# Splitting the loads at the end: the last w2 chunk in four loads of 51, 51, 16 and 10 rows

## The chip, the cores and the metric

The kernel runs on one core of a Trainium2 chip. The time is that of the whole program on the device, in microseconds (us); of several runs the median is taken. Beside the times there is a profile of one execution, with a trace of every instruction and of the packets that the core's 16 DMA engines moved.

## The reference

The reference is one decode step of an adaptive-layernorm transformer block: batch 8, one token each, model width 512, all in float32. Attention has 32 query heads over 8 key-value heads of size 128, and looks at the last 2048 positions of a cache of 8192. The second half is a feed-forward block of width 1792 with a squared ReLU.

```python
W = min(4096, max(256, Sk // 4))                       # 2048 positions
q = (x @ wq).reshape(B, Sq, Hq, Dh).transpose(0, 2, 1, 3)
k = repeat(k_cache[:, :, Sk - W:, :], rep, axis=1)
v = repeat(v_cache[:, :, Sk - W:, :], rep, axis=1)
p = softmax(einsum("bhqd,bhkd->bhqk", q, k) * Dh ** -0.5)
attn = einsum("bhqk,bhkd->bhqd", p, v).transpose(...).reshape(B, Sq, Hq * Dh) @ wo
...
mod = silu(c) @ w_mod                                   # sa, ca, ga, sb, cb, gb
x = x + ga * attn(layernorm(x) * (1 + ca) + sa)
h = layernorm(x) * (1 + cb) + sb
r = relu(h @ w1 + b1)
out = x + gb * ((r * r) @ w2 + b2)
```

Nearly all the work is reading: K and V of the window are 134 MB, and the weights some 30 MB more.

## The kernel before

All large operands pass through one SBUF tensor, `home`, that is cut into four slots of 4 MB, and one slot `small` of 2 MB. The list `loads` gives the order: w_mod, wq, then K and V tiles by turns (16 of each, two per key-value head) with three wo tiles between them, then the last two V tiles, `tail` (the last wo tile and half of w1), the other half of w1, and w2. `pump()` issues the next load as soon as a slot of its size is free, and `done()` frees a slot and calls it. All these loads are issued by SP (L105, L110, L124, L128), so they stand in one queue in this order. The framework gives the loads of SP and ACT eight semaphores in turn; a load that comes round to a semaphore waits until the load that had it before has landed. Within a slot a load waits only for the work on the part that it overwrites.

The five small loads of x and c (`xc_in`, L68; the last quarter of the width in two) and the two of the biases b1 and b2 (L503, L504) are issued by ACT.

The loop over `s` does attention in a fixed order: VectorE transposes K tiles (L190), TensorE computes scores (L359), VectorE and ScalarE the softmax, and TensorE multiplies by V (`weighted`, L446), five steps behind. `weighted` takes a V tile in four quarters; the last V tile is loaded as a half and two quarters, so that TensorE may start on each part as it lands. `parts` and `gather` (L463 to L475) bring a head's output into the tile `oT`, and `project_o` (L486) multiplies it by wo.

After the loop everything is one chain. L569 to L595 form the residual x1, the second layernorm and its transposed input; L611 multiplies by w1; L619 to L623 make the squared ReLU, `rT`; L630 multiplies by w2. The product has 14 chunks f of 128 rows of w2 each, and four column groups of 128. Its weight tile holds row 14 p + f of w2 in partition p, chunk f, so that a load of one chunk is 128 partitions of 2 KB. The w2 load is cut along the chunks: 0 to 7, 8 and 9, 10 and 11, 12, 13. A matmul waits only for the load that holds its chunk. `spin(n)` (L566) issues n matmuls on the identity matrix into a PSUM tile that nobody reads; they keep TensorE busy while it would wait. Each float32 matmul of the program shows as two in the profile. L638 and L639 apply the gate and the residual, and L640 stores the result.

Of the kernel before, what the change touches and what calls it, by code (L numbers as in the profile page):

```python
# [19 lines left out]
def tile_adaln_cached_attention_mlp(  # L20
# [14 lines left out]
    nc = tc.nc  # L35
    P = 128
    B, HKV, SK, DH = k_cache.shape
    D = wq.shape[0]
# [25 lines left out]
    nc.vector.memset(xc_in, 0.0)  # L64
    for q in range(D // P):
        b = slice(32 * q, 32 * q + B)
        for x, y in ((0, 2),) if q < 3 else ((0, 1), (1, 2)):
            nc.scalar.dma_start(xc_in[b, x:y], xc[b, x:y])  # L68

    ident = consts.tile([P, P], F32, name="ident")  # L70
# [8 lines left out]
    big = NJ * DH  # L79
# [9 lines left out]
    def size_of(key):  # L89
        return "small" if key[0] in ("wo", "w1") or key == ("mod", 1) else "big"  # L90

    def load(key):
        kind, i = key
        held[key] = free[size_of(key)].pop(0)
        if key == ("wq", 0):
            return
        t = slots[size_of(key)][held[key]]
        if kind in "KV":

            hk, c = divmod(i, 2)  # L100
            v = k_cache[4 * c : 4 * c + 4, hk] if kind == "K" else v_cache[c::2, hk]
            v = v[:, SK - W :, :].rearrange("u (p j) d -> p u (j d)", j=NJ)
            cuts = (0, big // 2, big * 3 // 4, big) if key == ("V", 2 * HKV - 1) else (0, big)
            for x, y in zip(cuts, cuts[1:]):
                nc.sync.dma_start(t[:, x:y], v[..., x:y])  # L105
            return

        def rows(o, v):
            n = v.shape[1] * v.shape[2]
            nc.sync.dma_start(t[:, o : o + n].rearrange("p (a n) -> p a n", n=v.shape[2]), v)  # L110

        w1v = w1.rearrange("(p kc) n -> p kc n", p=P)

        def wo_rows(j):

            r = 2 * REP * DH
            return wo[j * r : (j + 1) * r, :].rearrange("(h p i) n -> p h (i n)", p=P, i=4)

        if kind == "wo":
            rows(0, wo_rows(i))  # L120
        elif kind == "mod":

            v = w_mod.rearrange("(p kc) n -> p (kc n)", p=P)
            nc.sync.dma_start(t, v[:, big:] if i else v[:, :big])  # L124
        elif kind == "wq":

            o = base[held["wq", 0]]
            nc.sync.dma_start(home[:, o : o + 2 * big], wq.rearrange("(p k) n -> p (k n)", p=P))  # L128
        elif kind == "tail":
            rows(0, wo_rows(HKV // 2 - 1))  # L130
            rows(big // 2, w1v[:, 0:2])
        elif kind == "w1":
            rows(0, w1v[:, 2:4])
        else:
            v = w2.rearrange("(p c) n -> p c n", p=P)
            for lo, hi in ((0, 8), (8, 10), (10, 12), (12, 13), (13, 14)):
                rows(D * lo, v[:, lo:hi])

    def slot(key, n, o=0):

        t = slots[size_of(key)][held[key]][:, o:]
        return t[:, : t.shape[1] // n * n].rearrange("p (a n) -> p a n", n=n)
# [9 lines left out]
    def pump():  # L152
        while at[0] < len(loads) and free[size_of(loads[at[0]])]:
            load(loads[at[0]])
            at[0] += 1
# [53 lines left out]
    lo = consts.tile([P, 1], F32, name="lo")  # L209
    hi = consts.tile([P, 1], F32, name="hi")  # L210
# [31 lines left out]
    for k in (2, 3, 4):  # L242
        n = 1 << k
# [27 lines left out]
    for i, last in enumerate((16, 8)):  # L271
        at_ = 0
        while at_ < last:
            kc, m = divmod(16 * i + at_, 6)
            n = min(4 - m if m < 4 else 6 - m, last - at_)
# [234 lines left out]
    for s in range(N + PV_LAG + 1):  # L510
        g, i = divmod(s, C)
        q, h = divmod(s, 2)
        v = s - PV_LAG
# [49 lines left out]
    def spin(n):  # L563

        for _ in range(n):
            nc.tensor.matmul(spin_ps, ident, ident[:, None, :].to_broadcast([P, 4, P]), start=True, stop=True)  # L566
# [57 lines left out]

    py = ps_m.tile([P, 512], F32, name="m_ps", tag="m_ps")
    nc.tensor.matmul(py[:, :P], qsel.rearrange("p q b -> p (q b)"), b2_in, start=True, stop=False)
    spin(3)
    for f in range(FC):
        for q in range(NQ):
            nc.tensor.matmul(  # L630
# [6 lines left out]
    y = work.tile([P, P], F32, name="y", tag="one_y", bufs=1)  # L637
# [39 lines left out]
```

## Time and profile before

| | |
|---|---|
| Time before, median of 3 runs | 393.93 us (393.89 to 394.06) |
| The profiled execution: its own time | 394.02 us |
| Its span, first to last instruction | 392.2 us |
| Mean granted TensorE clock | 0.89 |
| TensorE matmul (PE), busy | 255.1 us, 65% |
| VectorE (DVE), busy | 219.7 us, 56% |
| ScalarE (ACT), busy | 46.3 us, 12% |
| Load queue of SP (q1): bytes, share of 16 engines | 164.70 MB, 98.3% |
| Mean rate over the span | 421 GB/s |

The span lies inside the program's time: the execution took 1.8 us more than its span. Engines are PE (matmul), PEld (weight load of TensorE), DVE, ACT, POOL and SP; a trailing q names the engine's sequencer, which issues DMAs. In the timeline a row has start, duration, engine, line, operation, tiles, count, and in brackets how long the engine had been idle and what ended the idle time. In the windows a row has the stretch, its length, then busy time and count of PE, PEld, DVE, ACT and POOL, then the granted clock, the mean busy share of the 16 DMA engines, and GB/s. In the rows of queues there are packets, MB and share; in those of issues the tiles, the issuing engine, the count, the size of each and, where it is known, the median time from issue to landing; in those of waits who waited for whom, microseconds in total, times, and the longest.

### The profile page before, as it was taken

The numbers are of one execution on the slowest core, as the hardware profiler recorded it, in microseconds if no ns is written. First come the engines' busy times: TensorE is split into PE (matmuls) and PEld (weight loads), VectorE is DVE, ScalarE is ACT, GpSimd is POOL, SyncE is SP. The second block draws the span as 40 slices with busy tenths as digits, with TensorE's granted clock in tenths as the row PEclk, the third lists the DMA queues.
The fourth block names the chain that finished last, engine by engine and source line by source line (L and its number), as shares of the span: only waits on it lengthen the run. The fifth ranks groups of instructions, "written<-read, shape, count | busy, mean of one in ns | idle before, by whom it ended". The sixth has DMA issues, their size and how long they took to land.

```text
span 392.2 us, 4670 instructions
## 1 busy us (share of the span) xinstructions
PE 255.1 (65%) x2006; PEld 77.7 (20%) x2006; DVE 219.7 (56%) x315; ACT 46.3 (12%) x89; POOL 1.3 (0%) x8
## 2 busy tenths in 40 slices
PE   0091958879228973797384837873774828896796
PEld 0030211112002321222021202221221202233324
DVE  1261099889056835783582817780775457855222
ACT  0120011221003100310031003000201003004010
POOL 0000000000000000000000000000000000000000
PEclk9997789989859996999699688999796969998989
DMA  8999999999999999999999999999999999999994
GB/s 329 430 435 439 440 435 431 428 430 401 453 428 428 426 431 428 430 431 446 423 426 435 428 433 435 430 424 431 407 450 431 426 431 436 432 423 408 427 424 178
DMA packets 7685, 165.04 MB, mean 421 GB/s; under 512 B 832, under 2 KB 1008, under 8 KB 1520
## 3 DMA queue, kind: packets, MB, share of 16 engines
q1 hardware_dynamic: 7568, 164.70, 98.3%
q8 instruction: 16, 0.26, 0.3%
q10 hardware_dynamic: 96, 0.04, 0.0%
q14 instruction: 5, 0.04, 0.0%
HBM read 164.67 MB, written 0.07 MB: 420 GB/s over the span
## 4 chain that ended last, share of the span: by engine, by line
DMA 62%; PE 19%; DVE 16%; issue 2%; SPq 0%; ACT 0%; DVEq 0%; ACTq 0%
DMA home<-in_A_k_cache_dram 46%; DVE kT L190 12%; DMA home<-in_A_wq_dram 9%; PE s_ps L359 8%; DMA home<-in_A_wo_dram 7%; PE m_ps L304 3%; PE o_ps L446 2%; PE q_ps L566 1%; DVE pT L425 1%; PE wo_ps L486 1%; PE m_ps L630 1%; PE m_ps L611 1%; PE p_ps L390 1%; DVE qbd L322 1%; DVE pr L418 1%
## 5 line engine op out<-in xcount | busy, mean ns | idle before, releaser
L190 DVE STREAM_TRANSPOSE kT<-home 128x1024 f32<-128x1024 f32 x128 | 151.1, 1219 | 87.0 <-DMA home<-in_A_k_cache_dram 83.6
L359 PE MATMUL s_ps<-kT,qst 128*32 128x512 f32 x512 | 129.4, 1076 | 21.5 <-DVE kT L190 20.6
L446 PE MATMUL o_ps<-home,pT 128*32 128x256 f32 x1024 | 69.8, 396 | 11.1 <-DVE pT L425 9.6
L446 PEld LDWEIGHTS o_ps<-home,pT 128*32 128x32 f32 x1024 | 33.5, 116 | 101.2 <-issue 60.5
L375 PE MATMUL m_ps<-ident,mx 128*1 128x128 f32 x16 | 4.3, 364 | 59.8 <-DVE mx L373 59.8
L359 PEld LDWEIGHTS s_ps<-kT,qst 128*32 128x32 f32 x512 | 14.5, 116 | 41.5 <-DVE kT L190 33.2
L425 DVE STREAM_TRANSPOSE pT<-pr 128x2048 f32<-128x2048 f32 x8 | 18.2, 2272 | 1.0 <-ACT pr L408 1.0
L408 ACT ACTIVATE pr<-pr,own 128x512 f32<-128x512 f32 x16 | 17.9, 1233 | 0.3
L402 ACT ACTIVATE pr<-p_ps,nm 128x512 f32<-128x512 f32 x8 | 5.5, 688 | 97.1 <-DVE nm L399 97.1
L369 ACT COPY ss<-s_ps 128x512 f32<-128x512 f32 x8 | 4.7, 587 | 100.6 <-issue 72.4
L347 ACT COPY qst<-q_ps 32x128 f32<-32x128 f32 x32 | 8.2, 257 | 70.2 <-PE q_ps L336 69.9
L304 PE MATMUL m_ps<-home,h1T 128*32 128x512 f32 x64 | 10.0, 793 | 8.7 <-DMA home<-in_A_wq_dram 8.7
L375 PEld LDWEIGHTS m_ps<-ident,mx 128*1 128x1 f32 x16 | 0.7, 81 | 65.0 <-DVE mx L373 65.0
L224 PE MATMUL m_ps<-xsum,sel 128*128 128x1 f32 x2 | 0.6, 362 | 19.8 <-DVE xsum L222 19.8
L322 DVE COPY qbd<-m_ps 32x128 f32<-32x128 f32 x8 | 3.0, 372 | 18.1 <-PE m_ps L319 18.0
L390 PE MATMUL p_ps<-ss,perm 128*128 128x512 f32 x16 | 11.3, 794 | 0.0
L399 DVE TENSOR_SCALAR nm<-m_ps 128x1 f32<-128x1 f32 x8 | 1.3, 158 | 15.8 <-PE m_ps L395 15.8
L418 DVE TENSOR_SCALAR pr<-pr,own 128x512 f32<-128x512 f32 x16 | 9.2, 657 | 0.8 <-ACT pr L402 0.8
L202 DVE TENSOR_SCALAR e_sb<-e_sb 128x128 f32<-128x128 f32 x1 | 0.2, 226 | 14.4 <-ACT e_sb L201 14.4
L429 PE MATMUL m_ps<-zs,tsel 128*128 128x8 f32 x16 | 2.9, 252 | 8.1 <-DVE zs L420 8.1
L463 DVE TENSOR_SCALAR o_sb<-o_ps,bit 128x128 f32<-128x128 f32 x16 | 4.9, 304 | 4.9 <-PE o_ps L446 4.9
L373 DVE TENSOR_REDUCE mx<-s_ps 128x1 f32<-128x512 f32 x8 | 5.3, 662 | 3.8 <-ACT ss L369 3.8
(124 smaller groups left out, 125.8 us busy)
## 6 DMA issues: line engine op xcount, KB each, us to landing
home<-in_A_k_cache_dram SPq DMA_DIRECT2D x16, 4096.0 KB, 27.0
home<-in_A_v_cache_dram SPq DMA_DIRECT2D x15, 4096.0 KB, 20.0
small<-in_A_wo_dram SPq DMA_DIRECT2D x3, 2048.0 KB, 31.1
home<-in_w_mod_dram SPq DMA_DIRECT2D x1, 4096.0 KB, 12.5
small<-in_w_mod_dram SPq DMA_DIRECT2D x1, 2048.0 KB, 16.9
home<-in_A_v_cache_dram SPq DMA_DIRECT2D x1, 2048.0 KB
home<-in_A_v_cache_dram SPq DMA_DIRECT2D x2, 1024.0 KB, 21.2
home<-in_A_wo_dram SPq DMA_DIRECT2D x1, 2048.0 KB, 25.5
```

The costliest lines, as they stand in the source:

```text
L190: nc.vector.transpose(KTS[q, j][:, rows], k[:, rows, 32 * j : 32 * j + 32])
L304: nc.tensor.matmul(pqs[r][32 * g : 32 * g + 32, :], hT[:, kc, :], w[:, 4 * r + g, :], start=(kc == 0), stop=(kc == NQ - 1),)
L322: nc.vector.tensor_copy(qbd[b, 4 * r : 4 * r + 4, j].rearrange("p g (b t) -> p t g b", t=REP), pT_[b].rearrange("p (t g b) -> p t g b", t= ...
L347: nc.scalar.copy(own[b, :, :, i, 0], pq[b, :P].rearrange("p (c m t) -> p c m t", c=2, t=REP))
L359: nc.tensor.matmul(s_ps[0][32 * g : 32 * g + 32, :], qst[hk % 2][:, P * (4 * c + u) + 32 * j :][:, :32], kT[:, u], start=(c == 0 and j == ...
L373: nc.vector.tensor_reduce(mx, s_ps[0], axis=AX.X, op=ALU.max)
L390: nc.tensor.matmul(sp, perm, SS_.pop(hk), start=True, stop=True)
L402: nc.scalar.activation(pr.rearrange("p j x -> p (j x)"), SS_.pop(hk), AF.Exp, bias=nm, scale=SCALE, accum_out=z)
L408: nc.scalar.mul(X_[hk][..., w], pr, own[:, w : w + 1])
L418: nc.vector.tensor_scalar(X_[hk][..., w], pr, own[:, w : w + 1], None, op0=ALU.mult)
L425: nc.vector.transpose(PT_[hk].rearrange("p e j r -> p j e r"), X_.pop(hk).rearrange("p j x w -> p j (x w)"))
L446: nc.tensor.matmul(O_[n][32 * g : 32 * g + 32, : 2 * DH], PT_[hk][:, e, j : j + 2].rearrange("p j r -> p (j r)"), vt[:, j : j + 2, :].rear ...
```

## The change

Four things change; no arithmetic does.

- The last chunk of w2 (13) is loaded in four loads by partition: rows 0 to 50, 51 to 101, 102 to 117 and 118 to 127. The other chunks come in three loads: 0 to 7, 8 to 11, 12.
- The last V tile is loaded in two halves.
- The last of the four loads of x and c is no longer cut into two.
- `spin(3)` ahead of the w2 product becomes `spin(1)`.

The number of loads in the whole program stays the same: three more for w2's last chunk, one fewer for its other chunks, one fewer for V, one fewer for x and c.

```diff
-        for x, y in ((0, 2),) if q < 3 else ((0, 1), (1, 2)):
+        for x, y in ((0, 2),):
             nc.scalar.dma_start(xc_in[b, x:y], xc[b, x:y])
...
-            cuts = (0, big // 2, big * 3 // 4, big) if key == ("V", 2 * HKV - 1) else (0, big)
+            cuts = (0, big // 2, big) if key == ("V", 2 * HKV - 1) else (0, big)
             for x, y in zip(cuts, cuts[1:]):
                 nc.sync.dma_start(t[:, x:y], v[..., x:y])
...
             v = w2.rearrange("(p c) n -> p c n", p=P)
-            for lo, hi in ((0, 8), (8, 10), (10, 12), (12, 13), (13, 14)):
+            for lo, hi in ((0, 8), (8, 12), (12, 13)):
                 rows(D * lo, v[:, lo:hi])
+            lo = 0
+            for n in (51, 51, 16, 10):
+                nc.sync.dma_start(t[lo : lo + n, D * 13 : D * 14], v[lo : lo + n, 13])
+                lo += n
...
     nc.tensor.matmul(py[:, :P], qsel.rearrange("p q b -> p (q b)"), b2_in, start=True, stop=False)
-    spin(3)
+    spin(1)
```

## The prediction

> **What bounds the kernel now.** I read the queues of the page first, then the busy time by stage for the last microseconds, then the timeline there. The page says that the load queue is nearly always busy:
>
> ```profile
> q1 hardware_dynamic: 7568, 164.70, 98.3%
> q8 instruction: 16, 0.26, 0.3%
> q10 hardware_dynamic: 96, 0.04, 0.0%
> ```
>
> SP's queue (q1) keeps the 16 DMA engines busy for 98.3% of the span, so only its end can be shortened. The windows there give, in the last two columns, the mean busy share of the 16 engines and the rate:
>
> ```profile
> 384.00:385.00 1.00, 1.00 (x4) 0.41 (x3) 0.26 (x1) 0.00 (x0) 0.00 (x0) 1.00 0.98 381
> 385.00:386.00 1.00, 1.00 (x14) 0.35 (x16) 0.00 (x0) 0.00 (x0) 0.00 (x0) 1.00 0.66 262
> 386.00:387.00 1.00, 1.00 (x47) 1.00 (x42) 0.00 (x0) 0.00 (x0) 0.00 (x0) 1.00 0.53 211
> 387.00:388.00 1.00, 1.00 (x48) 1.00 (x42) 0.00 (x0) 0.00 (x0) 0.00 (x0) 1.00 0.49 186
> 388.00:389.00 1.00, 1.00 (x36) 0.58 (x24) 0.00 (x0) 0.00 (x0) 0.00 (x0) 1.00 0.10 20
> ```
>
> The reader is to see that the engines do not finish together. In 387 to 388 the share is 0.49: eight of sixteen still carry data and eight have nothing left. In 385 to 386 the eight that finish early are missing for 0.34 × 16 = 5.4 engine-microseconds, so they end at about 385.3 on average. The last slice holds 0.10 × 16 = 1.6 engine-microseconds, for eight engines 0.2 each: the late ones carry their last byte at about 388.2. So the early half ends about 2.9 us ahead.
>
> The q8 row gives a cause: 16 fetches of instructions, 0.3% of sixteen engines' 392.2 us, or about 1.2 us each on one engine. Two such fetches on each of eight engines make about 2.4 us. Every load gives all sixteen engines the same number of rows, so nothing makes this up again. The timeline of the end:
>
> ```profile
> 382.88 2.84 PE L566 MATMUL q_ps<-ident 128*128 128x512 f32 x6
> 383.98 0.28 DVE L623 SCALAR_TENSOR_TENSOR pr<-relu 128x112 f32<-128x112 f32 x1
> 385.65 3.41 PE L630 MATMUL m_ps<-home,pr 128*32 128x128 f32 x112
> 388.63 0.16 PEld L630 LDWEIGHTS m_ps<-home,pr 128*32 128x32 f32 x8 [0.21 <-DMA home<-in_B_w_dram]
> 389.13 0.29 DVE L638 TENSOR_TENSOR y<-m_ps,modC 128x128 f32<-128x128 f32 x1 [4.87 <-PE m_ps L630]
> 389.77 0.35 SPq L640 DMA_DIRECT2D out_dram<-y  x1
> ```
>
> The w2 product (L630) has its operand at 384.26 (L623) but starts at 385.65, behind the warm-ups of L566. It runs 14 chunks in 3.41 us, 0.244 each, ends at 389.06, and waits for data only ahead of its last chunk: 0.21 us, until the last load is reported at about 388.6, which is 0.4 behind the last byte. Two things thus end almost together, the late engines' data and a product that started late. From 389.06 on everything is a chain that the change leaves alone.
>
> **The change part by part.** First, the early edits. The vector c and x come in four ACT loads instead of five, which shifts by one place the semaphores that loads take in turn:
>
> ```profile
> 1.16 2.03 ACTq L68 DMA_DIRECT2D xc_in<-in_xc_dram  x5
> 1.64 36.69 DMA home<-in_A_wq_dram
> SPq L105 <- DMA home<-in_w_mod_dram: 11.2, 1, 11.2
> ```
>
> One issue of 0.4 us goes, and SP's 11.2 us wait ahead of the first K load moves or disappears; but the chain runs through the wq load until 38.33 whatever was issued behind it. I cost this at nothing; without the wq load as cover it would be worth 0.4 us at most either way.
>
> Second, V's last tile in two loads. PE then gets its third quarter together with its fourth:
>
> ```profile
> 370.05 0.19 DVE L475 TENSOR_TENSOR oT<-tr,rz 128x32 f32<-128x32 f32 x1
> 371.35 2.97 PE L486 MATMUL wo_ps<-home,oT 128*32 128x512 f32 x16 [1.82 <-DMA home<-in_A_wo_dram]
> 119.37 1.07 PE o_ps L446 x16
> ```
>
> A quarter tile is 16 of these matmuls, about 1.1 us by the last row. L475 ends at 370.24, and L486 waits for the wo load until 371.35: 1.1 us of cover, and half of 2.97 more because the first eight of L486's sixteen matmuls belong to the head before. So nothing; without the cover, up to 1.1 us.
>
> Third, two warm-ups fewer. They are four of the six matmuls at L566: 2.84 × 4/6 = 1.9 us. PE is free at about 383.8, and the w2 product may start when its operand is there (384.3) and its first load has landed. Below the last report at 388.6 lie six chunks of eight rows per engine. A row is 2 KB; an engine moves 186/(0.49 × 16) = 23.7 to 262/(0.66 × 16) = 24.8 GB/s, so 0.082 us a row. The first w2 load is therefore reported at 388.6 − 6 × 8 × 0.082 = 384.7. The product can start 0.95 us earlier, but this is worth something only as far as the data allow.
>
> Fourth, chunks 8 to 11 in one load. This is reported at 388.6 − 2 × 8 × 0.082 = 387.3. Behind it PE has six chunks, 6 × 0.244 = 1.46 us, so it cannot end before 388.8. This is a new bound, 0.26 ahead of 389.06.
>
> Fifth, the last chunk as 51, 51, 16 and 10 rows. How many engines does such a load use?
>
> ```profile
> DMA packets 7685, 165.04 MB, mean 421 GB/s; under 512 B 832, under 2 KB 1008, under 8 KB 1520
> xc_in<-in_xc_dram ACTq DMA_DIRECT2D x3, 8.0 KB
> xc_in<-in_xc_dram ACTq DMA_DIRECT2D x2, 4.0 KB
> pr<-in_B_b_dram ACTq DMA_DIRECT2D x1, 7.0 KB
> pr<-in_B_b_dram ACTq DMA_DIRECT2D x1, 2.0 KB
> ```
>
> ACT's seven loads have 5 × 8 + 2 × 4 = 48 rows; their queue, q10, counts 96 packets, so every row brings one closing packet of its own: eight rows went to eight engines, four rows to four. Of the 832 small packets 784 remain, 16 for each of SP's 49 loads. In all these shapes the engines divide the rows evenly. For 51 rows no row of the trace exists. The bounds are one engine (51 rows each time) and sixteen (four at most). The nearest rows have equal shares on at most sixteen engines, and the largest such divisor of 51 is 3: 17 rows each. I take that. [...]
>
> Three engines then carry 17 + 17 + 1 + 1 = 36 rows instead of 8, 28 × 0.082 = 2.3 us more; all others one or two, 0.5 us less. Which three? No view prints engine numbers. I followed the packet records behind the DMA column engine by engine: they run without gaps, so each can be followed, though near neighbours may be mixed up. The engines of the four-row loads are among those of the eight-row loads; three of the four are early and one is late; of the four others at least two are late. If engines are taken in order and the fetches fall on a block of neighbours, the block starts at the fourth engine, and the first three are early. Then they end at 385.3 + 2.3 = 387.6, at the worst of them 388.0, and the others at 388.2 − 0.5 = 387.7. With 0.4 for the report and 0.24 for the chunk, PE ends by this at 388.25 to 388.65, ahead of the bound of 388.8.
>
> The sum: PE ends at 388.8 instead of 389.06, −0.26. The profiled execution took 394.02 us (span 392.2 and 1.8 around it), 0.09 above the median of 393.93; so 393.76 on its scale and 393.7 on that of the runs.
>
> The added issues, three more on SP for the last chunk, wait for older loads:
>
> ```profile
> 378.87 1.71 PE L611 MATMUL m_ps<-home,pr 128*32 128x448 f32 x16
> 361.86 4.88 SPq L110 DMA_DIRECT2D home<-in_B_w_dram  x5
> SPq L110 <- DMA home<-in_A_v_cache_dram: 15.6, 4, 8.8
> SPq L640 <- DMA home<-in_A_wo_dram: 4.6, 1, 4.6
> home<-in_B_w_dram SPq DMA_DIRECT2D x2, 256.0 KB, 22.2
> out_dram<-y SPq DMA_DIRECT2D x1, 64.0 KB, 1.6
> ```
>
> L640 shows it: eight semaphores go round, and the store already waits for the wo load, eight places ahead. Now the sixth and seventh w2 loads would wait for the wo load (371.3) and the first w1 load (in use by L611 at 378.87). Only the store is queued behind them, which needs y at 389. They are issued by about 379, for data due at 387: nothing. A load on an idle queue lands 1.6 us after issue, so the cover is some 6 us.
>
> [...] Here the 22.2 us from issue to landing say that start-up lies under queued data.
>
> **The rivals.** *One of the three is a late engine.* It decides as soon as any of the three is in the half that ends at 388.2. Then 28 rows more end at 388.2 + 2.3 = 390.5, reported at 390.9, PE ends at 391.15: +2.1, or 396.0. For it: half of all engines are late, and one of the four. Against it: the order just described. 0.27.
>
> *The load is spread evenly after all*: at most 4 + 4 + 1 + 1 = 10 rows, 0.16 later, 394.1; the change does not do what it says. 0.05.
>
> *PE becomes slow*: with fewer warm-ups the clock drops, and six chunks at half speed cost 1.46 more: PE ends at 390.3, 1.2 later than before, about 395.1. Against it:
>
> ```profile
> 370.00:372.00 2.00, 0.66 (x8) 0.29 (x12) 0.20 (x2) 0.00 (x0) 0.00 (x0) 1.00 1.06 451
> ```
>
> PE was idle here for 1.3 of 2 us at a granted clock of 1.00; the new gaps are under 1 us. 0.03.
>
> *Each small load pays its own start*, 3 × 1.6 = 4.8: 398.7. 0.02. One engine for 51 rows, 94 × 0.082 = 7.7 more at least: over 401. 0.01.
>
> *The early engines have more room*: if chunks 8 to 11 land 0.6 earlier than I put it, PE ends by the last chunk, and 0.8 is gained: 393.1. 0.04.
>
> **How the numbers follow.** The forecast itself has 0.58. A measurement of this kernel can tell about 0.2%, 0.8 us, from no change. Forecast and even spread are within that: 0.63. Late engine, slow PE, start-up and single engine are slower: 0.33. Faster: 0.04. The forecast's own range is 393.4 to 394.1, from the landing of chunks 8 to 11 (0.3 either way) and the worst early engine. That leaves out more than 2 in 10, so the range goes on to the late engine, 396.2.
>
> **What would show it.** Right: the DMA share in the last 2 us below 0.49 with three engines or fewer in the very end; L630 starting near 384.7, waiting for w2 near 387.3, ending near 388.8; L486 still released by the wo load; two matmuls at L566. Wrong: a DMA share near 3/16 or less for about 2 us with L630 waiting in it, which is a late engine; more than one wait of over 0.5 us ahead of the last chunk; matmuls of L630 longer than before; an SP wait for the first w1 load that lasts beyond 385.

## The result and the profile after

The kernel after takes 395.06 us (median of 10 runs, 394.76 to 395.67), the kernel before 394.06 in the same session (10 runs, 393.89 to 394.35): a ratio of 1.0026, 95% interval 1.0016 to 1.0036. It is slower by 1.0 us, more than the 0.2% that can be told from no change. The forecast was 393.7; the range to 396.2 holds the result. A few single executions, of the kernel before among others, took 397.4 to 398.7 us where the rest of the same kernel's lie near 394; no median rests on them.

The profiled execution took 395.34 us (span 393.4), 1.32 more than the one of before. First the windows of after, with the columns as before (share of the DMA engines and GB/s last):

```profile
385.00:386.00 1.00, 0.69 (x26) 0.72 (x29) 0.00 (x0) 0.00 (x0) 0.00 (x0) 1.00 0.77 258
386.00:387.00 1.00, 1.00 (x48) 1.00 (x39) 0.00 (x0) 0.00 (x0) 0.00 (x0) 1.00 0.68 195
387.00:388.00 1.00, 0.27 (x12) 0.00 (x0) 0.00 (x0) 0.00 (x0) 0.00 (x0) 1.00 0.66 201
388.00:389.00 1.00, 0.81 (x32) 0.81 (x32) 0.00 (x0) 0.00 (x0) 0.00 (x0) 1.00 0.21 64
389.00:390.00 1.00, 0.58 (x24) 0.34 (x17) 0.00 (x0) 0.00 (x0) 0.00 (x0) 1.00 0.09 18
```

The reader is to see the last two columns together. In 386 to 387 the share is 0.68 where it was 0.53: 2.4 engines more are busy, as the prediction wanted of the three that take the rows of the last chunk. But they move 195 GB/s, not 211. A busy engine carries 195/(0.68 × 16) = 17.9 GB/s; before, it was 24.9. More engines work and less arrives. The timeline of the product (L634, where before has L630) and of the store:

```profile
385.31 1.95 PE L634 MATMUL m_ps<-home,pr 128*32 128x128 f32 x64 [1.91 <-DMA home<-in_B_w_dram]
388.19 1.30 PE L634 MATMUL m_ps<-home,pr 128*32 128x128 f32 x40 [0.92 <-DMA home<-in_B_w_dram]
389.91 0.43 PE L634 MATMUL m_ps<-home,pr 128*32 128x128 f32 x8 [0.42 <-DMA home<-in_B_w_dram]
391.04 0.38 SPq L644 DMA_DIRECT2D out_dram<-y  x1
```

PE is idle three times for data: 1.91 us ahead of chunk 0, 0.92 ahead of chunk 8, 0.42 ahead of chunk 13. It ends at 390.34 instead of 389.06, +1.28; the store follows 1.27 later than before. So the whole loss of this execution lies in the landing of w2.

### The profile page after: what moved, and what is told of

Its sections match the earlier page's. It is cut to its first block, busy times and chain, and to the rows that moved or that the text cites. A ratio compares the mean times of both kernels' runs of the same rounds, so it can differ in the third digit from the quotient of the medians.

```text
span 393.4 us, 4662 instructions
## 1 busy us (share of the span) xinstructions
PE 250.1 (64%) x2002; PEld 75.9 (19%) x2002; DVE 219.6 (56%) x315; ACT 46.2 (12%) x89; POOL 1.3 (0%) x8
## 4 chain that ended last, share of the span: by engine, by line
DMA 75%; DVE 12%; PE 11%; issue 1%; SPq 0%; DVEq 0%
DMA home<-in_A_k_cache_dram 55%; DMA home<-in_B_w_dram 11%; DVE kT L194 10%; DMA home<-in_A_wq_dram 9%; PE s_ps L363 7%; PE m_ps L308 2%; PE o_ps L450 2%; DVE qbd L326 1%; DVE o_sb L468 1%; DVE o_sb L467 0%; SPq L124 0%; PE m_ps L323 0%; PE m_ps L634 0%; DVE y L642 0%; DVE y L643 0%
## 5 line engine op out<-in xcount | busy, mean ns | idle before, releaser
L450 PE MATMUL o_ps<-home,pT 128*32 128x256 f32 x1024 | 69.2, 392 | 11.3 <-DVE pT L429 9.6
L308 PE MATMUL m_ps<-home,h1T 128*32 128x512 f32 x64 | 8.6, 700 | 10.6 <-DMA home<-in_A_wq_dram 10.6
```

The costliest lines, as they stand in the source:

```text
L308: nc.tensor.matmul(pqs[r][32 * g : 32 * g + 32, :], hT[:, kc, :], w[:, 4 * r + g, :], start=(kc == 0), stop=(kc == NQ - 1),)
L450: nc.tensor.matmul(O_[n][32 * g : 32 * g + 32, : 2 * DH], PT_[hk][:, e, j : j + 2].rearrange("p j r -> p (j r)"), vt[:, j : j + 2, :].rear ...
```

## The experiments

The theory after the two traces: **shared write side**. DMA engines that write into the same few partitions slow one another, as if they shared something, which the expectation below calls a path. It is the author's guess from the two windows (195 GB/s at a share of 0.68, 211 at 0.53); what would be shared, and by which partitions, they do not show. By it, three engines that carry 102 rows write into partitions that the late engines still write too, and slow them. The rivals: **start-up** (each small load costs something by itself), **merge** (chunks 8 to 11 in one load are to blame), and the warm-ups.

**The parts alone.** First, the kernel before with the split only:

```diff
-            for lo, hi in ((0, 8), (8, 10), (10, 12), (12, 13), (13, 14)):
+            for lo, hi in ((0, 8), (8, 10), (10, 12), (12, 13)):
                 rows(D * lo, v[:, lo:hi])
+            lo = 0
+            for n in (51, 51, 16, 10):
+                nc.sync.dma_start(t[lo : lo + n, D * 13 : D * 14], v[lo : lo + n, 13])
+                lo += n
```

> Kernel before with one edit: the last w2 chunk in four loads of 51, 51, 16 and 10 rows. Shared write side (two or more DMA engines that write into the same few partitions share one path, so the 102 rows of the three engines run at about 0.11 us a row, not 0.082, and the other engines' packets slow down too, as the trace of after shows with 195 GB/s at a share of 0.68 against 211 at 0.53): the last chunk is reported 0.7 to 1.2 us later than before, +0.7 to +1.2 us. Merge (chunks 8 to 11 in one load are to blame): 0, within 0.3. Start-up (each small load costs something by itself): +1.0, as in after.

Measured: 395.34 us (5 runs) against 394.02, ratio 1.0037 (1.0023 to 1.0050): 1.3 us, a little above the range of the theory. Second, the kernel after with chunk 13 in one load, `((0, 8), (8, 12), (12, 13), (13, 14))`:

> Kernel after with the last chunk in one load of 128 rows; everything else of after stays. Shared write side: the last chunk is reported at about 388.6 as before, chunks 8 to 11 at about 387.3, a DMA share and GB/s as in before (0.53 at 211 in 386 to 387); 0 to -0.3 us against before. Merge: +0.7 to +1.2. Start-up: 0 to -0.3, as shared write side.

Measured: 394.22 (11 runs), ratio 1.0006 (0.9997 to 1.0014). Third, the kernel before with `spin(1)` for `spin(3)`:

> Kernel before with one warm-up call instead of three, nothing else. If PE is bound by the last chunk's report at 388.6: 0, within 0.2 us, with the product starting at about 384.7 and a wait for w2 ahead of the last chunks. If the start at 385.65 was part of the bound: -0.3 to -0.6. If fewer warm-ups lower the clock: +1.

Measured: 394.10 (11 runs), ratio 0.9999 (0.9979 to 1.0019). The split makes the whole loss, and the rest of the change is worth nothing that can be measured. Merge falls. The timeline says how the split does it. The kernel with one warm-up, whose product starts early enough to show every landing; these are the waits ahead of chunks 10, 12 and 13:

```profile
387.33 0.38 PEld L630 LDWEIGHTS m_ps<-home,pr 128*32 128x32 f32 x16 [0.27 <-DMA home<-in_B_w_dram]
387.97 0.16 PEld L630 LDWEIGHTS m_ps<-home,pr 128*32 128x32 f32 x8 [0.27 <-DMA home<-in_B_w_dram]
388.61 0.16 PEld L630 LDWEIGHTS m_ps<-home,pr 128*32 128x32 f32 x8 [0.48 <-DMA home<-in_B_w_dram]
```

The same three waits in the kernel with the split alone:

```profile
388.06 0.38 PEld L634 LDWEIGHTS m_ps<-home,pr 128*32 128x32 f32 x16 [0.94 <-DMA home<-in_B_w_dram]
388.76 0.16 PEld L634 LDWEIGHTS m_ps<-home,pr 128*32 128x32 f32 x8 [0.33 <-DMA home<-in_B_w_dram]
389.26 0.19 PEld L634 LDWEIGHTS m_ps<-home,pr 128*32 128x32 f32 x8 [0.34 <-DMA home<-in_B_w_dram]
```

The reader is to see that chunk 13 is not alone: chunks 10 and 11, loaded as before, are 0.73 late, chunk 12 0.79, chunk 13 0.65. These wait for the late engines, which carry no more rows than before. They have been slowed, and the packet records of the traces say so directly: of the 4 KB packets (rows of chunks 8 to 11) that start between 385.5 and 387, the median took 0.20 us with the split alone and 0.16 before.

**Partitions by themselves.** A kernel that only loads: rows of 28 KB, each load waited for before the next, the same rows into different partitions.

```diff
+    def phase(*parts):
+        t = pool.tile([P, 7168], F32, name="t", tag="t")
+        for rows, to in parts:
+            nc.sync.dma_start(t[to], v[rows])
+    phase((slice(0, 8), slice(0, 8)))
+    phase((slice(0, 8), slice(0, 32, 4)))
...
```

> Leaves the whole computation out and stores zeros: twelve loads of 28 KB rows, each waited for before the next, the whole list twice: 128 rows; 8 rows into partitions 0 to 7, into every fourth, into every sixteenth; 16 rows into 0 to 15, into every eighth; 32 rows into 0 to 31, into every fourth; 51 rows into 0 to 50, into every second; 3 rows into 0 to 2, into 0, 4 and 8. An engine alone needs 28.7 KB / 24.9 GB/s = 1.15 us a row, a load on an idle queue lands about 1.7 us after that. [...] No shared write side: 8 rows 2.9 wherever they go, 16 rows 2.9, 32 rows 4.0, 3 rows 2.9. [...]

Its timeline; the bracket is the time from the end of one phase to the landing of the next, in the order of the expectation, from 128 rows to 3 rows side by side:

```profile
11.88 0.14 DVE L53 COPY sink<-t 1x1 f32<-1x1 f32 x1 [10.89 <-DMA t<-in_B_w_dram]
17.60 0.14 DVE L53 COPY sink<-t 1x1 f32<-1x1 f32 x1 [5.58 <-DMA t<-in_B_w_dram]
21.55 0.14 DVE L53 COPY sink<-t 1x1 f32<-1x1 f32 x1 [3.80 <-DMA t<-in_B_w_dram]
26.20 0.14 DVE L53 COPY sink<-t 1x1 f32<-1x1 f32 x1 [4.51 <-DMA t<-in_B_w_dram]
32.21 0.14 DVE L53 COPY sink<-t 1x1 f32<-1x1 f32 x1 [5.87 <-DMA t<-in_B_w_dram]
36.75 0.14 DVE L53 COPY sink<-t 1x1 f32<-1x1 f32 x1 [4.41 <-DMA t<-in_B_w_dram]
43.48 0.14 DVE L53 COPY sink<-t 1x1 f32<-1x1 f32 x1 [6.58 <-DMA t<-in_B_w_dram]
48.58 0.14 DVE L53 COPY sink<-t 1x1 f32<-1x1 f32 x1 [4.96 <-DMA t<-in_B_w_dram]
76.96 0.14 DVE L53 COPY sink<-t 1x1 f32<-1x1 f32 x1 [28.23 <-DMA t<-in_B_w_dram]
100.49 0.14 DVE L53 COPY sink<-t 1x1 f32<-1x1 f32 x1 [23.39 <-DMA t<-in_B_w_dram]
105.41 0.14 DVE L53 COPY sink<-t 1x1 f32<-1x1 f32 x1 [4.78 <-DMA t<-in_B_w_dram]
```

Eight rows take 5.58 us side by side and 3.80 into every fourth partition, but 4.51 into every sixteenth, though those lie further apart. So the partitions alone change the time, and their distance alone does not explain it; which partitions slow one another is not shown. Sixteen rows take 5.87 side by side and 4.41 spread, 32 rows 6.58 and 4.96, three rows 4.78, and 3.50 into partitions 0, 4 and 8. The start costs more than I put (3.80 where 2.9 was expected). Fifty-one rows side by side take 28.23 us, longer than 128 (10.89), and longer than the 21 that 17 rows of 1.15 us behind one another and 1.7 would make; into every second partition they take 23.39. The windows of the two:

```profile
55.00:70.00 15.00, 0.00 (x0) 0.00 (x0) 1.00 0.18 59
80.00:95.00 15.00, 0.00 (x0) 0.00 (x0) 1.00 0.19 75
```

0.18 × 16 = 2.9: about three engines, each at 59/2.9 = 20 GB/s; spread out, 0.19 × 16 = 3.0 engines have 75/3.0 = 25 each.

The second kernel of this kind loads all 128 rows in pieces, queued one behind another.

```diff
+    for n in (7168, 512):
+        for _ in range(2):
+            phase(n, slice(0, 128))
+            phase(n, *blocks(32, 32, 32, 32))
+            phase(n, *combs(4))
+            phase(n, *blocks(64, 64))
+            phase(n, *combs(2))
+            phase(n, *blocks(51, 51, 16, 10))
```

> Leaves the whole computation out and stores zeros: 128 rows loaded six ways, each waited for, the list twice with rows of 28 KB and twice with rows of 2 KB: one load; four blocks of 32; four combs of 32 (every fourth partition); two blocks of 64; two combs of 64; 51, 51, 16 and 10. [...] Rows of 2 KB: 0.66 us of data; one load 2.3; shared write side: blocks of 32 up to 3, combs 2.3 to 2.6; start-up: blocks and combs alike, 3.3 to 3.8; 51/51/16/10 about 36 x 0.082 + 1.7 = 4.7 in both.

The windows within the load of 128 rows, four blocks of 32, four combs of 32, two blocks of 64, and 51/51/16/10, for rows of 28 KB:

```profile
2.00:10.00 8.00, 0.00 (x0) 0.00 (x0) 1.00 0.87 373
14.00:30.00 16.00, 0.00 (x0) 0.00 (x0) 1.00 0.99 204
34.00:42.00 8.00, 0.00 (x0) 0.00 (x0) 1.00 0.92 380
46.00:62.00 16.00, 0.00 (x0) 0.00 (x0) 1.00 0.98 204
80.00:125.00 45.00, 0.00 (x0) 0.00 (x0) 1.00 0.21 68
```

This is the clearest line of the study. Blocks and combs are as many loads of as many rows on as many engines, all of them busy (0.99 and 0.92), and the blocks move 204 GB/s where the combs move 380. If a small load only cost something by itself, the two would be alike. The median packet of 28 KB took 2.23 us in the blocks and 1.06 in the combs. The totals: 11.2 us for one load, 20.1 for blocks of 32, 11.3 for combs, 20.3 for blocks of 64, 11.6 for two combs, 52.2 for 51/51/16/10. For rows of 2 KB on an idle queue start-up counts as well (one load took 2.8 us, of which the data are an estimated 0.66): 2.8, 3.4, 4.3, 3.5, 3.3 and 5.5; here the combs are not the faster ones, against both theories.

**The same three engines, other partitions.** The last step was to show it in the kernel. Eight kernels are the kernel before plus useless loads of three rows behind the last w2 chunk, into a part of `home` that nobody reads any more; they differ in the partitions alone (and the last in the amount). Partitions 0, 16, 64 and 80 came first; 112, 96, 84 and half the data at 80 were added when 80 had come out dear:

```diff
     project_o(HKV - 1)
+    e, v = home[:, base[free["big"][0]] :], w2.rearrange("(p c) n -> p c n", p=P)
+    for i in range(4):
+        nc.sync.dma_start(e[80:83, 2048 * i : 2048 * i + 2048].rearrange("p (a n) -> p a n", n=D), v[0:3, 0:4])
```

> Kernel before with four useless loads behind the last w2 chunk, of three rows of 8 KB each, into partitions 0 to 2 of a part of the buffer that nobody reads any more. Three engines carry 32 KB each, 1.3 us, behind their own rows (from about 385.3), while the late engines are still at the last chunks until 388.2. The four kernels of this kind differ only in the partitions: 0, 16, 64 or 80 and the two behind each. [...] No shared write side: all four alike, within 0.2 us of before. [...]

> As the kernel with partitions 0 to 2, but the useless rows go to partitions 16 to 18. [...]

> As the kernel with partitions 0 to 2, but the useless rows go to partitions 64 to 66. [...]

> As the kernel with partitions 0 to 2, but the useless rows go to partitions 80 to 82. [...]

> As the kernel with useless rows in partitions 80 to 82 (398.06), but in 112 to 114. [...]

> [...]

> [...]

> As the kernel with useless rows in partitions 80 to 82 (398.06), with two such loads instead of four, 48 KB instead of 96. Shared write side: about half the cost, +1.2 to +2.5 us. An accident of that kernel or a cost that does not go with the data: 0, or +4 as before.

| partitions of the useless rows | median (lowest to highest) | before beside it |
|---|---|---|
| 0 to 2 | 394.35 (394.20 to 397.45) | 394.04 |
| 16 to 18 | 394.74 (394.24 to 395.48) | 394.04 |
| 64 to 66 | 394.36 (394.20 to 394.48) | 394.04 |
| 96 to 98 | 394.49 (394.22 to 398.67) | 394.02 |
| 80 to 82 | 398.06 (396.58 to 398.16) | 394.04 |
| 112 to 114 | 398.15 (397.85 to 398.22) | 394.02 |
| 84 to 86 | 397.93 (397.77 to 398.16) | 394.02 |
| 80 to 82, half the data | 395.40 (394.66 to 395.87) | 394.02 |

At 0, 64 and 96 the rows cost 0.3, 0.3 and 0.5 us, which the scatter covers, at 16 0.7; at 80, 84 and 112 they cost 4.0, 3.9 and 4.1 (ratio at 112: 1.0100, 1.0084 to 1.0117); half the data at 80 costs 1.4. So the same rows, in loads of the same shape, are cheap or dear by their partitions alone, and the price goes with the data. What makes a partition dear these kernels do not show. The window 386 to 387 with the rows at 64:

```profile
386.00:387.00 1.00, 1.00 (x46) 1.00 (x39) 0.00 (x0) 0.00 (x0) 0.00 (x0) 1.00 0.71 234
```

With the rows at 80, and the product's long wait:

```profile
386.00:387.00 1.00, 1.00 (x45) 0.94 (x36) 0.00 (x0) 0.00 (x0) 0.00 (x0) 1.00 0.75 90
...
390.97 1.03 PE L633 MATMUL m_ps<-home,pr 128*32 128x128 f32 x24 [2.75 <-DMA home<-in_B_w_dram]
```

At 64 the three early engines, (0.71 − 0.53) × 16 = 2.9, add 234 − 211 = 23 GB/s to what before moved. At 80 0.75 × 16 = 12 engines are busy and all of them together move 90 GB/s, and chunk 10 waits until 390.97. If only the three with the useless rows were slow, the nine others would still move an estimated 9 × 24.9 = 224, at their rate in before. They have 10 GB/s each at most: engines that carry none of the useless rows are slowed too. The packet records show it packet by packet: from 386 to 388 there are 32 packets of 4 KB, the work of about eight engines, and every one took 0.44 to 0.62 us; with the rows at 64 they took 0.16 to 0.17, as before. Why they are slowed no run shows.

**Place or number of loads?** Two kernels with one warm-up came first, the kernel after with four loads of 32 rows for its split, as blocks and as combs:

```diff
-            for n in (51, 51, 16, 10):
+            for n in (32, 32, 32, 32):
```

> Kernel after with the last chunk in four loads of 32 rows each instead of 51, 51, 16 and 10: as many loads, but eight rows for each of the 16 engines. [...] Start-up: +1.0, as after. Merge: +0.7 to +1.2.

```diff
+            for i in range(4):
+                nc.sync.dma_start(t[i:P:4, D * 13 : D * 14], v[i:P:4, 13])
```

> Kernel after with the last chunk in four loads of 32 rows, every fourth row each, instead of 51, 51, 16 and 10; the loads of 32 neighbouring rows took 395.58 us. [...] Start-up of each load: 395.4 to 395.6, as with neighbouring rows.

Measured: blocks 395.58 (ratio 1.0036, 1.0024 to 1.0049), as much as the threes; combs 394.93 (1.0022, 1.0013 to 1.0031). The blocks' profile holds a second thing, a granted clock (third column from the end) of 0.50:

```profile
386.00:387.00 1.00, 1.00 (x28) 1.00 (x23) 0.00 (x0) 0.00 (x0) 0.00 (x0) 0.50 0.51 199
...
384.88 4.98 PE L634 MATMUL m_ps<-home,pr 128*32 128x128 f32 x112 [1.84 <-DMA home<-in_B_w_dram]
```

The product took 4.98 us instead of 3.41 and hid the landings. So both were run again on the kernel before, with three warm-ups, and beside them seven w2 loads of 128 rows, `((0, 8), (8, 9), (9, 10), (10, 11), (11, 12), (12, 13), (13, 14))`:

> Kernel before (three warm-ups, chunks 8 to 11 in two loads) with the last chunk in four loads of 32 neighbouring rows. [...] Number of loads: +1.0 to +1.5. If the 395.58 of the kernel with one warm-up was mostly the clock: below +0.5.

> Kernel before with the last chunk in four loads of 32 rows, every fourth row each; three warm-ups. [...] Number of loads: the same as the blocks, within 0.2.

> Kernel before with seven w2 loads instead of five, all of 128 rows: chunks 8, 9, 10 and 11 in a load each instead of two by two. [...] Shared write side: 0, within 0.3 us. Number of loads: +0.6 to +1.2 (two loads more, of the 0.3 to 0.6 each that the two more of after would then have cost).

Measured against 394.10: blocks 395.35 (1.0031, 1.0019 to 1.0042), combs 394.89 (1.0020, 1.0011 to 1.0030), seven whole loads 394.33 (1.0015, 0.9996 to 1.0034). The waits ahead of chunks 10, 12 and 13 with blocks:

```profile
388.01 0.38 PEld L632 LDWEIGHTS m_ps<-home,pr 128*32 128x32 f32 x16 [0.82 <-DMA home<-in_B_w_dram]
388.64 0.16 PEld L632 LDWEIGHTS m_ps<-home,pr 128*32 128x32 f32 x8 [0.25 <-DMA home<-in_B_w_dram]
389.44 0.19 PEld L632 LDWEIGHTS m_ps<-home,pr 128*32 128x32 f32 x8 [0.64 <-DMA home<-in_B_w_dram]
```

With combs:

```profile
387.38 0.38 PEld L632 LDWEIGHTS m_ps<-home,pr 128*32 128x32 f32 x16 [0.27 <-DMA home<-in_B_w_dram]
388.03 0.16 PEld L632 LDWEIGHTS m_ps<-home,pr 128*32 128x32 f32 x8 [0.28 <-DMA home<-in_B_w_dram]
388.85 0.19 PEld L632 LDWEIGHTS m_ps<-home,pr 128*32 128x32 f32 x8 [0.66 <-DMA home<-in_B_w_dram]
```

Blocks hold up chunks 10 and 12 by 0.7, combs leave them where the unsplit kernel has them (387.33, 387.97). That is the place. In the profiled executions PE ends at 389.90 with blocks and 389.31 with combs, 389.06 before, so place is the larger part of the delay; the intervals of the two ratios overlap, and the reading rests on these rows. It is not all: the blocks' 1.25 us lies within the 1.0 to 1.5 of the number of loads, and the combs, which hold up neither of these chunks, still cost 0.8. Nor is it the number of loads alone, by which the combs would be within 0.2 of the blocks.

The combs' own chunk 13 is still 0.24 late. Slower packets do not explain it: from 387 on the 2 KB packets of the combs took 0.08 to 0.09 us, as in the kernel with one warm-up, and the last of them ended at 388.22, where that kernel has 388.13. Most of the delay comes behind the last byte. From the end of the last w2 packet to the start of chunk 13 the nine kernels read that have the chunk in one load took 0.46 to 0.51 us; the five that have it in four and don't hide it took 0.63 to 0.75, after 0.75. That the product then waits for four reports instead of one fits this; no run tests it.

A second cost of more loads seems to lie behind the store. From the issue of the store to the end of the span before took 2.43 us, and after, with as many loads, 2.36. The twelve kernels with two to four loads more took 2.6 to 3.0, among them the split alone with 2.68 and the seven whole loads with 2.65. In the combs' profile (2.99) more of the loss lies there than ahead of the store. It is not a clean sign: the kernel with one warm-up has as many loads as before and took 3.55, its store landing late. What makes this cost stays open. No version run here is faster than before.

## Why the prediction was wrong, point by point

- *The engines end unevenly, and the early ones have room.* Right. Useless rows on three engines cost 0.3 us at partitions 0 and 64; at 64 the share in 386 to 387 was 0.71 instead of 0.53, and the product ended on time, at 389.03. That fetches of instructions make some engines late is not tested by any run.
- *The edits of x, c and V cost nothing.* Right: the kernel that has them and not the split is at 394.22, not to be told from before. In after, the wo product still starts with its load:

```profile
371.63 1.92 PE L490 MATMUL wo_ps<-home,oT 128*32 128x512 f32 x16 [1.45 <-DMA home<-in_A_wo_dram]
```

- *Two warm-ups fewer let the product start earlier, worth only what the data allow.* Right: worth nothing (394.10).
- *Chunks 8 to 11 reported at 387.3.* Right only while the last chunk is whole. This is that kernel, ahead of chunks 8 and 13:

```profile
387.46 1.03 PEld L630 LDWEIGHTS m_ps<-home,pr 128*32 128x32 f32 x40 [0.67 <-DMA home<-in_B_w_dram]
...
388.73 0.16 PEld L630 LDWEIGHTS m_ps<-home,pr 128*32 128x32 f32 x8 [0.24 <-DMA home<-in_B_w_dram]
```

In after it was 388.19. The bound of 388.8 that carried the forecast moved with it.
- *Fifty-one rows go to three engines, and these are early.* Right: 2.9 engines in the kernel that only loads, and the rows at partitions 0 and 64 ran in the early engines' free time. That the late engines are a block from the fourth on was the author's guess, and no run shows it. Nor do the early engines make a load cheap everywhere: the useless rows cost 3.9 to 4.1 us at 80, 84 and 112, 0.3 to 0.5 at 0, 64 and 96, and 0.7 at 16.
- *28 rows more at 0.082 us, and all other engines 0.5 us less.* **This step failed**, in both halves. The price of a row was taken from loads of 128 rows; three engines by themselves, with 51 rows side by side, have 20 GB/s each, 0.10 us a row of 2 KB. And the other engines did not end at 387.7: with the split alone the chunks that they carry come 0.7 us late, though they have fewer rows. The last packet of w2 ended at 389.14 in after (388.50 with the split alone), where 387.6 to 388.0 was put. Moving rows to an idle engine does not take them out of the way of the others: the useless rows, in loads of one shape, cost 0.3 or 4.0 us by their partitions alone. The trace of before could not show it, since all its large loads have 128 rows. A smaller term was mis-sized too: the 0.4 us from the last packet to the report holds for a chunk in one load (0.46 in before up to the start of chunk 13), in after it was 0.75.
- *The rivals.* None of them had this mechanism. "One of the three is a late engine" gave 396.0 and a right-looking sign (slower), but the three are early. Spread evenly: no. Each small load pays 1.6 us (the row that this came from is the store's): no, the split costs 1.3 in all. PE at a slower clock: not in after. But the row that was put against it, 370 to 372 at a clock of 1.00 with PE mostly idle, says less than was read from it: in 372 to 374 of the same trace the granted clock was 0.52, and L486 took 2.97 us where after's L490 took 1.92 at a clock of 1.00. That drop came behind an idle stretch of 1.82 us that ended at 371.35; in the first kernel with four blocks one came behind 1.84 us (0.50 from 385 to 388).
- *The issues of SP.* Nothing shows that they cost: most of the split's delay appears in chunks 10 to 12 already, whose loads are issued before it.

## What to carry to other kernels

In these runs a DMA engine that is idle is not free bandwidth: the same three-row loads cost 0.3 us into partitions 64 to 66 and 4.0 into 80 to 82. Ahead of splitting a load by rows, ask which partitions the other engines are still writing, and time the split at those partitions. Cut along the free dimension into seven loads of 128 rows, w2 left the kernel at 394.33 us against 394.10; the last chunk in blocks of 32 rows made it 395.35. Loads of every fourth row slowed no other load here (chunks 10 and 12 at 387.38 and 388.03), but still cost 0.8 us. The sign in a profile is a DMA share that rises while GB/s falls (0.53 to 0.68, 211 to 195).

## What was not expected of the hardware

- 96 KB of useless data into three partitions cost 4.0 us; at the 25 GB/s that one engine had in before, all of it one behind another would take an estimated 3.9 us. Chunk 10 came at 390.97, 3.6 later than in the kernel with one warm-up; with 48 KB at 388.95, 1.6 later. A part of the end is clock and not data: from 390 to 391 the granted clock was 0.50 with the rows at 112 and 0.69 with those at 84, and the last 32 matmuls took 1.94 us in both. From 386 to 387 all busy engines together move 90 GB/s. Why engines that carry none of the useless rows slow down too is not shown.
- Two blocks of 64 rows are no faster than four of 32, both at 204 GB/s, a little over half of the 373 of one load of 128 rows. What makes them alike is not shown.
- Once, with PE idle for 1.84 us ahead of the product, the granted clock was 0.50 for three us; after and three other kernels waited as long (1.91, 1.81, 1.84, 1.81) at a clock of 1.00. With waits of 2.82 and 3.20 us ahead of chunk 10 (rows at 84 and 112) it was 0.69 and 0.50 from 390 to 391. With one of 2.75 us (rows at 80) it was still 1.00 there, but the last eight matmuls, from 392.17, took 0.63 us where the kernel with one warm-up took 0.43. What decides it stays open.
